# Lightning attention with a leaky-ReLU feed-forward part: a third couple of feature pairs by seven products, and a new order of the group pairs

## The chip, the cores and the metric

The kernel runs on one core of a Trainium2 chip. The metric is the device time of one execution in microseconds; the median of three runs of the kernel before is 598.87 us (598.29 to 600.73).

## What is computed

The reference is an attention with decay, by blocks of 64 positions, whose output goes through two matrix products with a leaky ReLU between:

```python
# q, k, v: (4, 8, 768, 64) float32; lam: (8,)
intra = einsum('bhic,bhjc->bhij', qb, kb) * Dmask        # Dmask = lam ** (i - j) for i >= j
out[:, :, sl] = einsum('bhij,bhjd->bhid', intra, vb) + einsum('bhid,bhde->bhie', qb * lam_pow, kv_state)
kv_state = lam ** 64 * kv_state + einsum('bhsd,bhse->bhde', kb * rev_pow, vb)
...
x = attn_out.transpose(0, 2, 1, 3).reshape(3072, 512)
h = x @ w_in                    # w_in (512, 2048)
out = maximum(0.01 * h, h) @ w_out   # w_out (2048, 512)
```

The two products are 3072x512x2048 and 3072x2048x512. In the kernel each operand of a large product is split into three parts (`h`, `l`, `m`) of a reduced float format, and each product is three passes of TensorE over 128x128 weights and 512 columns.

## The kernel before, in words

**Tiling.** The 3072 tokens are 24 chunks of 128; four chunks are a group (six groups, 0 to 5), two groups are a pair of groups (0-1, 2-3, 4-5; `pr` 0, 1, 2). The 2048 features are eight pairs of 128 (`p` 0 to 7, "feature pairs"); two feature pairs are a couple (`u`: 0 is pairs 0 and 1, 1 is pairs 2 and 3).

**Stages.** The attention's rounds (`round_of`, L552), one a chunk, run between blocks of the first product (`up`, L711; matmuls in L723): a block is one group by one feature pair, 24 matmuls, and ends in ACT passes (L742, L747) into a buffer `gs`. What happens to it then depends on the feature pair. For a *plain* pair the block is written to DRAM (`G`, L754). For a pair that goes *by seven products* `sums` (L777) forms three sums or differences of its token and feature halves on DVE (L783) and writes six kinds of blocks to DRAM (`BB`, L791).

The second product follows, one pair of groups after another. It reads the blocks back as **units** (`unit`, L809): one load of 512 KB by SP (L825), an ACT pass (L828) and two DVE passes (L831, L835) that split 128x1024 values into three parts in one of five **ring slots**. A slot is used again five units later, when PE is done with it. A plain unit (`plain`, L885) is one feature pair of one group, 24 matmuls (L851). By Strassen's scheme (`strassen`, L854) a couple of feature pairs and a pair of groups take seven products of 12 matmuls each, numbered 1 to 7 in the code; a product is one unit. Each product adds into one of four couples of PSUM banks, X, Y, Z or V (`KINDS`, L804); between products ACT copies a couple (`copy_banks`, L958) or ACT and DVE add one to another (`add_banks`, L962; L965, L966), through the staging buffer `w32`. Product 4 has a second load and one more DVE pass (L842, L843) through the same `w32`.

The products need sums of weights: an operand for product 5 stands in the place of a quarter of the weights, and three more for products 6, 7 and 3 stand in "extra" places that the attention's buffers left (`w_sums`, L684; `more`, L670). There is room for those of feature pairs 0 to 3. So before, feature pairs 0 and 1 of the first pair of groups and 0 to 3 of the other two go by seven products (`NS, NS0 = 4, 2`, L203), the rest plain.

**What sets the order.** The work is listed in `seq`, written out by hand; an item's place is its rank. `Plan` then orders each engine's queue at build time from costs and latencies written beside each operation: at each step it takes the operation that can start first, and among equals the one of lowest rank. Units of the second product have their rank lowered by `LEAD` items, so that they are ready ahead. TensorE may take a later item when an earlier one is not ready, as far as the banks allow. All ordinary loads and stores go out on SP in that one order; the output's stores (`store_out`, L951) on ACT's queue, the last ones also on SP. For a pair of groups the list is, with `s(t, u)` for product t of couple u and `n(p, gi)` for a plain unit:

```python
seq += [late[0], s(1, 0), late[1], s(1, 1), ("copy", "Z", "X"), late[2], s(6, 0), late[3], s(6, 1), ("copy", "Y", "Z"),
        s(5, 0), s(5, 1), ("add", "Y", "V"), s(7, 0), s(7, 1), ("add", "V", "Z"),
        s(3, 0), n(4, 0), s(2, 0), n(5, 0), s(3, 1), s(2, 1), n(6, 0), s(4, 0), s(4, 1), n(7, 0)]
```

`late` are the four plain units of the second group of the pair before, moved in between. The last two plain units make the ending (L917).

## Time and profile before

| | |
|---|---|
| median of 3 runs | 598.87 us |
| profiled execution | 598.83 us, of which span 597.1 us |
| granted TensorE clock | 1.0 |
| attention and first product | to 349 us, mixed with the first products of pair 0-1 from 324 us |
| pair 0-1 | last plain units to 437 us, mixed with the first products of pair 2-3 from 413 us |
| pair 2-3 | last plain units to 519 us, mixed with the first products of pair 4-5 from 494 us |
| pair 4-5 | to 592.6 us, then the last stores |
| DMA | 123.04 MB, 206 GB/s over the span |

The page of the profile gives each engine's busy time; its chain of work shows what each instruction on the way to the end waited for. A line such as `437.04 2.77 PE po L851 x12` is start, length, engine, tile written, line of the kernel and count. The names of tiles: `psc` are the banks X, `po` Z, `b` and `pt` are Y and V; `xh`, `xl`, `xm` and `raws` are ring slots, `w` is `w32` or a weight, `att`, `attb` and `lows` are the attention's buffers that later hold sums of weights.

### The profile page before, as it was taken

How to read it: one execution, taken by the hardware profiler on the slowest of the kernel's cores; microseconds unless marked ns; L12 is line 12 of the kernel's file. 1: busy time of each engine (PE TensorE's matmuls, PEld its weight loads, DVE VectorE, ACT ScalarE, POOL GpSimd, SP SyncE). 2: the span in 40 equal slices, each digit the busy share in tenths (PEclk: the TensorE clock that was granted, in tenths of full speed). 3: DMA queues.
4: the chain of work that ended last, by engine and by line, in shares of the span. 5: the costliest groups of instructions: out<-in, count | busy, mean ns of one | idle time of the engine just before them, and what ended most of it. 6: DMA issues, size and time to landing. Idle time of an engine off the chain costs nothing.

```text
span 597.1 us, 13281 instructions
## 1 busy us (share of the span) xinstructions
PE 586.2 (98%) x5336; PEld 485.0 (81%) x5336; DVE 406.7 (68%) x559; ACT 299.2 (50%) x468; POOL 134.0 (22%) x170
## 2 busy tenths in 40 slices
PE   7899999999999999999999999999999999999997
PEld 6778888888888888888788888888888888888886
DVE  4999883357365565465389889965689695788652
ACT  3788884345555565565598874331344223252300
POOL 2654770835636348121000000000000000000000
PEclk9999999999999999999999999999999999999999
DMA  8999855975899999886788865526467547394533
GB/s 205 238 292 242 245 171 132 247 195 132 240 284 260 239 269 232 247 259 224 244 273 273 298 196 206 162 89 190 128 198 223 175 144 193 121 259 164 177 107 70
DMA packets 163949, 123.04 MB, mean 206 GB/s; under 512 B 100400, under 2 KB 140592, under 8 KB 163888
## 3 DMA queue, kind: packets, MB, share of 16 engines
q1 hardware_dynamic: 148128, 112.75, 64.4%
q10 hardware_dynamic: 13200, 5.77, 3.8%
q0 software_dynamic: 2560, 3.68, 2.5%
q8 instruction: 42, 0.69, 0.5%
q14 instruction: 19, 0.16, 0.1%
HBM read 81.27 MB, written 40.89 MB: 205 GB/s over the span
## 4 chain that ended last, share of the span: by engine, by line
PE 91%; DVE 5%; DMA 2%; ACT 0%; issue 0%; SPq 0%; DVEq 0%
PE b L723 43%; PE po L851 13%; PE b L851 12%; PE psc L851 11%; PE pt L851 4%; PE po L335 4%; PE psc L335 3%; DMA xm<-g 1%; DVE wl L628 1%; DVE w L617 1%; DMA attb<-in_q_dram 1%; DVE w L616 1%; PE pt L425 1%; DVE att L474 0%; DVE xl L530 0%
## 5 line engine op out<-in xcount | busy, mean ns | idle before, releaser
L723 PE MATMUL b<-xh,wh 128*128 128x512 f32 (+2 forms) x392 | 103.6, 387 | 0.8 <-ACT xh L529 0.8
L723 PE MATMUL b<-xm,wm 128*128 128x512 f32 (+2 forms) x392 | 103.7, 393 | 0.0
L723 PE MATMUL b<-xl,wl 128*128 128x512 f32 (+2 forms) x392 | 103.5, 386 | 0.1
L828 ACT ACTIVATE xh<-xm 128x1024 fp32r<-128x1024 f32 x46 | 48.8, 1060 | 86.6 <-DMA xm<-g 40.9
L723 PEld LDWEIGHTS b<-xh,wh 128*128 128x128 f32 x392 | 72.7, 188 | 16.1 <-ACT xh L529 0.9
L723 PEld LDWEIGHTS b<-xl,wl 128*128 128x128 f32 x392 | 72.8, 188 | 15.2 <-DVE wl L628 0.5
L723 PEld LDWEIGHTS b<-xm,wm 128*128 128x128 f32 x392 | 71.2, 188 | 15.1 <-ACT b L742 0.4
L742 ACT ACTIVATE b<-b 128x512 f32<-128x512 f32 (+2 forms) x97 | 56.1, 581 | 54.5 <-PE b L723 54.4
L747 ACT ACTIVATE gs<-b 128x512 f32<-128x512 f32 (+2 forms) x97 | 56.8, 591 | 39.7 <-PE b L723 34.6
L831 DVE SCALAR_TENSOR_TENSOR xl<-xm,xh 128x1024 fp32r<-128x1024 f32 x46 | 56.0, 1218 | 26.4 <-ACT xh L828 25.5
L835 DVE SCALAR_TENSOR_TENSOR xm<-xl,xh 128x1024 fp32r<-128x1024 f32 x50 | 61.2, 1224 | 3.5
L484 POOL TENSOR_TENSOR att<-att 128x256 f32<-128x256 f32 x40 | 34.9, 873 | 37.9 <-DVE att L481 37.9
L616 DVE TENSOR_SCALAR w<-w 128x512 int32<-128x512 int32 x32 | 22.6, 706 | 27.2 <-ACT w L610 27.1
L396 POOL DMA_DIRECT2D attb<-in_q_dram x64 | 39.5, 624 | 2.9 <-issue 1.4
L445 POOL TENSOR_TENSOR att<-att 128x512 f32<-128x512 f32 (+1 forms) x20 | 24.9, 1244 | 63.4 <-PE po L335 47.4
L441 POOL TENSOR_TENSOR attb<-attb,att 128x512 f32<-128x512 f32 (+1 forms) x23 | 26.1, 1136 | 34.6 <-PE po L425 10.5
L851 PE MATMUL psc<-xm,wm 128*128 128x512 f32 x84 | 32.8, 391 | 0.1
L851 PE MATMUL psc<-xh,wh 128*128 128x512 f32 x84 | 32.7, 389 | 0.0
L851 PE MATMUL psc<-xl,wl 128*128 128x512 f32 x84 | 32.7, 389 | 0.0
L474 DVE TENSOR_TENSOR att<-psc,att 128x512 f32<-128x512 f32 x24 | 16.5, 688 | 21.9 <-PE psc L335 21.8
L617 DVE CUSTOM_DVE_ANT_0 w<-w,lows 128x1024 uint16<-128x1024 uint16 x32 | 26.2, 818 | 7.1 <-ACT lows L614 6.2
L828 ACT ACTIVATE raws<-raws 128x1024 fp32r<-128x1024 f32 x12 | 12.7, 1061 | 27.6 <-DMA raws<-g 18.1
(184 smaller groups left out, 1096.3 us busy)
## 6 DMA issues: line engine op xcount, KB each, us to landing
xm<-b SPq DMA_DIRECT2D x28, 512.0 KB, 3.8
g<-gs SPq DMA_DIRECT2D x27, 512.0 KB, 4.6
xm<-g SPq DMA_DIRECT2D x22, 512.0 KB, 4.2
b<-gs SPq DMA_DIRECT2D x20, 512.0 KB, 3.9
raws<-in_moe_w_in_dram SPq DMA_DIRECT2D x16, 512.0 KB, 5.2
raws<-in_moe_w_out_dram SPq DMA_DIRECT2D x16, 512.0 KB, 4.9
attb<-in_k_dram SPq DMA_DIRECT2D x48, 128.0 KB, 4.7
attb<-in_v_dram SPq DMA_DIRECT2D x24, 256.0 KB, 4.7
```

The source lines that it names most:

```text
L335: nc.tensor.matmul(dst[HALF[cols]], lhsT=lhsT[HALF[rows]], rhs=rhs[HALF[rows]], start=start, stop=True, skip_group_check=True)
L396: (move if nm == "k" else carry)(0.55 if nm == "k" else QSL, lambda o=o, z=z, e=nc.sync if nm == "k" else nc.gpsimd: e.dma_start(out=o.rea ...
L484: add("POOL", 0.7, lambda new=new, j=j: nc.gpsimd.tensor_tensor(state[(j + 1) % 4], new, _bc(lam_c, 2, D), op=ALU.mult), [f"st{j % 4}", "f ...
L616: add("DVE", 0.42, lambda: nc.vector.tensor_scalar(d, d, 3, None, op0=ALU.logical_shift_left), [], [key])
L617: add("DVE", 1.0, lambda: nc.vector.tensor_tensor(d, d, low, op=ALU.add), [kl], [key])
L723: nc.tensor.matmul(dst, lhsT=w[z][:, kk * 2 * P + f * P:kk * 2 * P + (f + 1) * P], rhs=x[z][:, kk, toks], start=start and kk == 0, stop=kk ...
L742: add("ACT", ns, lambda b=b: nc.scalar.activation(out=b, in_=b, func=AF.Copy, bias=0.0, scale=S + 1.0), [], [kb], rank=-1.5)
L747: add("ACT", t, lambda o=o, x=s_: nc.scalar.activation(out=o, in_=x, func=AF.Prelu, bias=0.0, scale=(1.0 + 1.0 / S) / (WS * U), alpha=0.01 ...
L828: nc.scalar.activation(out=ring[j][0], in_=g(), func=AF.Copy, bias=0.0, scale=NEAR)
L831: nc.vector.scalar_tensor_tensor(ring[j][1], g(), 1.0, ring[j][0].bitcast(F32), op0=ALU.mult, op1=ALU.subtract)
L835: nc.vector.scalar_tensor_tensor(m, l.bitcast(F32), -S, h.bitcast(F32), op0=ALU.mult, op1=ALU.add)
L851: nc.tensor.matmul(dst, lhsT=lhs(z), rhs=ring[j][z][:, col:col + n], start=first and z == 0, stop=z == 2, skip_group_check=True)
```

## The change

Three things are changed.

1. In one pair of groups, 2-3, three couples (feature pairs 0 to 5) go by seven products: `NSP = [2, 6, 4]`. Feature pairs 6 and 7 stay plain.
2. The pairs of groups are worked through in the order 0-1, 4-5, 2-3, so that this pair comes last. The sums of weights of feature pairs 4 and 5 are formed during pair 4-5 (`w_apart`, items `wq`), in a ring slot, and written to DRAM (`ES`). In the last pair they are fetched (`fetches`, items `wd`) into places whose last use is over: the first weight quarter of feature pairs 0 to 3 (after product 1), one extra place (after product 6), two unused ends of the extra buffers, and the quarter of feature pairs 4 and 5 themselves that product 5 replaces (after their late plain units). Each fetch is 128 KB; there are 24.
3. `seq`, the order of the feature pairs in `up`, and the planner's constants are new.

```diff
     NS, NS0 = 4, 2
+    NSP = [2, 6, 4]
...
-    LEAD = 8.0
+    LEAD = 6.0
...
-    HOLD, WPR, WSR, LEAD0 = 0.15, 2.0, 0.0, 12.0
+    HOLD, WPR, WSR, LEAD0 = 0.6, 8.0, 8.0, 10.0
...
+    ES = {p: dram.tile([P, 6 * d_model], F32, name=f"es{p}", tag=f"es{p}") for p in range(NS, max(NSP))}
...
+    def apart(z, p, k):
+
+        if p == NS or k == 0:
+            return W[k if p == NS else 3][z][:, :NQ]
+        if k == 2:
+            return more(z, 0)[:, :NQ]
+        return extra["lows"][:, 3 * NQ:] if z == 2 else extra["attb"][:, NB - (2 - z) * NQ:NB - (1 - z) * NQ]
+
+    def w_apart(p):
+
+        nonlocal n_ring
+        j, n_ring = RING[(n_ring - len(slots)) % NR], n_ring + 1
+        k, r = ["w320", "w321"], [f"r{z}{j}" for z in "hlm"]
+        add("DMA", 1.5, lambda: nc.sync.dma_start(out=w32f, in_=WO[p]), [f"WO{p}0", f"WO{p}1"], k)
+        b = [w32f[:, i * NQ:(i + 1) * NQ] for i in range(4)]
+        for o, x, y, op in ((3, 1, 3, ALU.add), (1, 0, 1, ALU.subtract), (0, 3, 0, ALU.subtract), (2, 2, 0, ALU.subtract)):
+            add("DVE", 0.42, lambda o=o, x=x, y=y, op=op: nc.vector.tensor_tensor(b[o], b[x], b[y], op=op), [], k)
+        add("ACT", 1.05, lambda: nc.scalar.activation(out=ring[j][0], in_=w32f, func=AF.Copy, bias=0.0, scale=NEAR / S), k, r[:1])
+        add("DVE", 1.25, lambda: nc.vector.scalar_tensor_tensor(ring[j][1], ring[j][0].bitcast(F32), -S, w32f, op0=ALU.mult, op1=ALU.add),
+            k + r[:1], r[1:2])
+        add("DVE", 1.25, lambda: nc.vector.tensor_tensor(ring[j][2], ring[j][1].bitcast(F32), ring[j][0].bitcast(F32), op=ALU.subtract), r[:2], r[2:])
+        add("ACT", 1.06, lambda: nc.scalar.activation(
+                out=ring[j][2], in_=ring[j][2].bitcast(F32), func=AF.Copy, bias=0.0, scale=1.0 / (S + 1.0)), [], r[2:])
+        for z in range(3):
+            add("DMA", 1.5, lambda z=z: nc.sync.dma_start(out=ES[p][:, z * 2 * d_model:(z + 1) * 2 * d_model], in_=ring[j][z].bitcast(F32)), r[z:z + 1], [f"ES{p}{z}"])
+
+    def fetch(p, k, to, writes):
+        for z in range(3):
+            add("DMA", 0.5, lambda z=z: nc.sync.dma_start(out=to(z).bitcast(F32), in_=ES[p][:, (z * 4 + k) * NQ:(z * 4 + k + 1) * NQ]),
+                [f"ES{p}{z}"], [w.format("hlm"[z]) for w in writes])
+
+    def fetches(i):
+
+        if i == 2:
+            for p in (NS, NS + 1):
+                fetch(p, 3, lambda z, p=p: W[p][z][:, NQ:2 * NQ], [f"w{{}}{p}"])
+            return
+        for p, k in ((4, 0), (5, 0), (4, 1), (5, 1), (4, 2)) if i == 0 else ((5, 2),):
+            fetch(p, k, lambda z, p=p, k=k: apart(z, p, k), [f"E{p}{k}{{}}"])
...
-            for i, f in enumerate(fs if p < (NS if g > 1 else NS0) else [None]):
+            for i, f in enumerate(fs if p < NSP[g // 2] else [None]):
...
-    ORDER = [4, 0, 3, 7, 2, 6, 5, 1]
+    ORDER = [0, 3, 2, 7, 1, 5, 4, 6]
...
-    for pr in range(NG // 2):
+
+    for pr, before in ((0, None), (2, 0), (1, 2)):
...
+            if pr == 2:
+                seq += [
+                    late[0], late[1], s(1, 0), ("wq", 4), s(1, 1), ("copy", "Z", "X"), late[2], late[3], s(6, 0), s(6, 1),
+                    ("copy", "Y", "Z"), s(5, 0), s(5, 1), s(7, 1), ("add", "Y", "V"), s(7, 0), s(2, 1), ("add", "V", "Z"),
+                    n(4, 0), s(3, 0), n(5, 0), s(3, 1), s(4, 1), s(2, 0), n(6, 0), s(4, 0), n(7, 0), ("wq", 5)]
+            else:
+                seq += [
+                    late[2], late[1], s(1, 0), s(1, 1), s(1, 2), late[0], late[3], ("wd", 0), ("copy", "Z", "X"), s(5, 0),
+                    s(6, 2), s(6, 1), s(5, 1), ("wd", 2), s(6, 0), s(5, 2), ("copy", "Y", "Z"), ("wd", 1), ("add", "Y", "V"),
+                    s(7, 2), s(7, 0), s(7, 1), s(2, 0), ("add", "V", "Z"), n(6, 0), s(3, 0), s(3, 2), s(2, 1), s(4, 0),
+                    s(2, 2), s(3, 1), s(4, 2), s(4, 1), n(7, 0)]
...
-            put(("up", NG - 1, 2), ("ws", 0))
+            put(("up", NG - 1, 1), ("ws", 0))
             put(("up", NG - 1, 2), ("ws", 1))
-            put(("up", NG - 1, 6), ("fr",))
+            put(("up", NG - 1, 4), ("fr",))
```

The list of the first part of `seq` is new too: up to `("wi", 3)` it is the old one; after it the weights of feature pair 4 come earlier, those of 7 and 0 a little later, and some blocks of `up` change places. The plain units of pair 0-1 also stand in another order.

More of the change, by code (lines that the diff above doesn't have):

```diff
@@ L667, in operand @@
             return W[p][z][:, t * NQ:(t + 1) * NQ]
-        return more(z, p)[:, (-1 - t) * NQ:-t * NQ]
+        return more(z, p)[:, (-1 - t) * NQ:-t * NQ] if p < NS else apart(z, p, -1 - t)
     def more(z, p):
@@ L750, in up @@
         plan.ahead = 0.0
-        if p >= (NS if g > 1 else NS0):
+        if p >= NSP[g // 2]:
             d = G[g // 2][p].rearrange("p (f h g t) -> p f h g t", f=2, h=2, g=2)
@@ L881, in strassen @@
         begins = pr == 0 and t == 1
-        add("PE", 0.227 * (13 if begins else 12), go, [f"r{z}{j}" for z in "hlm"] + [f"{'w' if w >= 0 else 'e'}{z}{p}" for z in "hlm" for p in ps_],
+        add("PE", 0.227 * (13 if begins else 12), go, [f"r{z}{j}" for z in "hlm"] + [f"w{z}{p}" if w >= 0 else f"e{z}{p}" if p < NS else f"E{p}{-1 - w}{z}" for z in "hlm" for p in ps_]
+            + [x + z for x in (["E40", "E41", "E42", "E50"] if t == 1 and u < 2 else ["E52"] if t == 6 and u == 0 else []) for z in "hlm"],
             ACC[d] + (ACC["Z"] if begins else []))
@@ L994, in n @@
             return ("n", r, p, gi) if p < NP - 1 else ("l", r, p, gi, (0, 1, 2, 3) if gi == 0 else (2, 3, 0, 1))
-        late = [n(p, 1, pr - 1) for p in range(NS, NP)] if pr else []
+        late = [n(p, 1, before) for p in range(NS, NP)] if pr else []
         if pr:
-            seq += [late[0], s(1, 0), late[1], s(1, 1), ("copy", "Z", "X"), late[2], s(6, 0), late[3], s(6, 1), ("copy", "Y", "Z"),
-                    s(5, 0), s(5, 1), ("add", "Y", "V"), s(7, 0), s(7, 1), ("add", "V", "Z"),
-                    s(3, 0), n(4, 0), s(2, 0), n(5, 0), s(3, 1), s(2, 1), n(6, 0), s(4, 0), s(4, 1), n(7, 0)]
+            if pr == 2:
[9 more added lines that the diff above has]
+                    s(2, 2), s(3, 1), s(4, 2), s(4, 1), n(7, 0)]
         else:
@@ L1046 @@
             w_sums(x[1])
+        elif x[0] == "wq":
+            w_apart(x[1])
+        elif x[0] == "wd":
+            fetches(x[1])
         elif x[0] == "fr":
```

15 lines of the change are left out of this document (8 added, 7 removed), and 5 rows, old and new, of the table seq.

## Prediction

> **What bounds the kernel now.** I read the page's busy shares first, then the table of windows, then PE's waits, then the chain of work in order of time, and last the DVE and SP timelines of one pair of groups.
>
> ```profile
> PE 586.2 (98%) x5336; PEld 485.0 (81%) x5336; DVE 406.7 (68%) x559; ACT 299.2 (50%) x468; POOL 134.0 (22%) x170
> ```
>
> PE is nearly always busy, but a mean says nothing of stages. The table of windows does (columns: window, its length, busy us of PE, PEld, DVE, ACT, POOL with counts, granted clock, DMA share, GB/s):
>
> ```profile
> 0.00:35.00 35.00, 29.46 (x654) 23.47 (x654) 26.45 (x53) 20.57 (x37) 15.98 (x22) 1.00 0.91 228
> 35.00:60.00 25.00, 24.56 (x354) 19.98 (x348) 23.93 (x32) 21.26 (x37) 12.07 (x10) 1.00 0.98 266
> 60.00:292.00 232.00, 232.00 (x3000) 193.46 (x2998) 129.23 (x233) 129.97 (x230) 106.00 (x140) 1.00 0.81 223
> 292.00:360.00 68.00, 67.60 (x311) 55.43 (x312) 56.38 (x75) 55.89 (x86) 0.00 (x0) 1.00 0.82 269
> 360.00:437.04 77.04, 77.04 (x341) 63.79 (x340) 58.20 (x61) 25.07 (x29) 0.00 (x0) 1.00 0.48 149
> 437.04:518.80 81.76, 81.76 (x361) 67.60 (x361) 62.52 (x59) 27.48 (x30) 0.00 (x0) 1.00 0.59 180
> ```
>
> From 60 us to the last pair PE is full: 232.00 of 232.00, 77.04 of 77.04, 81.76 of 81.76. All the room there is before the end lies ahead of 35 us (5.54 us), in 35 to 60 (0.44) and in 292 to 360 (0.40). PE's waits say what it is:
>
> ```profile
> PE psc L335 <- DVE att L481: 1.8, 2, 1.1
> PE b L282 <- POOL att L285: 1.4, 1, 1.4
> PE b L723 <- ACT xh L529: 0.8, 1, 0.8
> PE po L425 <- DVE xl L530: 0.7, 1, 0.7
> ```
>
> These are start-up waits of the attention part. So the kernel is bound by the number of matmuls; anything on another engine is free as long as PE does not wait for it.
>
> **The removed work.** The chain in order of time shows one product of the seven (12 matmuls of 128x512) and two of them in a row:
>
> ```profile
> 437.04 2.77 PE po L851 x12
> ...
> 445.25 5.49 PE po L851 x24
> 450.74 2.72 PE b L851 x12
> ```
>
> A product is 2.72 us, 0.2267 us a matmul. Before, feature pairs 4 and 5 of groups 2 and 3 take 2 x 2 plain units of 24 matmuls: 96, or 21.76 us. After, they are a third couple in each of the seven products: 7 x 12 = 84, or 19.04 us. **12 matmuls less: -2.72 us.** Nothing else on PE changes in number: the other couples, the `up` blocks, the two extra zeroing matmuls of the first product and the ending stay. The saving cannot fail to exist; it can only be eaten by waits.
>
> Beside this row the Trainium skill ("Perfetto Trace Analysis", Identifying the Most-Contended Engine) calls matmul busy time a bad measure and wants the share of weight loads, here 81%. Read so, PE would have 19% room and twelve matmuls might vanish in it (a rival below). The trace speaks against it: a load takes 0.188 us and the next matmul starts 0.2267 us after the last, and 0.188/0.2267 is 83%, so the 81% is that ratio and not idle time.
>
> **The added work, and what hides it.** A "unit" is one 128x1024 operand: one 512 KB load, one ACT pass (1.06 us, L828), two DVE passes (1.22 each, L831 and L835), into one of five ring slots. The last pair has 7 x 3 + 4 = 25 units instead of 22, and three of product 4 (one more load and one more DVE pass, 1.22).
> - DVE, last pair with the four late units before it: 27 units x 2.44 = 65.9, product 4 3 x 1.22 = 3.7, the two bank sums 4 x 0.69 = 2.8, eight output transposes 5.6: 78.0 us, beside PE's 21 x 2.72 + 6 x 5.44 = 89.8. That is 87%, where the pair at 437 us has 62.5 of 81.8 (76%). Hidden on the whole.
> - The weight sums (`w_apart`, twice, in the pair before): 4 x 0.42 + 2 x 1.22 = 4.1 us of DVE, 2.1 of ACT, one load and three stores of 512 KB, and a ring slot each. DVE there becomes 62.5 + 8.3 = 70.8 of 81.8. The slot is held about load 5.4 + DVE and ACT 6.2 + store 4.6 = 16 us; four units stand before its next user, two of them plain ones of 5.44, so 16.3 us. Cost taken: 0; without that cover about one unit's latency less the rest, some 2 us.
> - Sums of activations: 3 x 0.42 us of DVE (L783) for four more blocks in groups 2 and 3, 5 us in a stage where DVE is busy 129 of 232. They stand ahead of the attention's own DVE steps, which have 11 us of other PE work in each round to hide in. Cost 0; upper bound 5.
> - `up` order, ranks and the order of pairs (0-1, 4-5, 2-3): same instructions. Before 35 us the order is the same. After it, it can win at most the 0.44 + 0.40 us of idle time, and it can lose: in 320 to 330 DVE is busy 9.83 of 10 us. I take 0, bounds -0.8 and +3.
>
> **Long runs of products.** The pair now has ten products in a row (from product 5 of couple 0 to product 2 of couple 0), one plain unit, then eight. In a run each unit must be ready within four products, 10.88 us from the release of its slot. The six-run before shows it for product 3 (its load, its two passes with a bank sum between, from the SP and DVE timelines; PE starts it at 450.74):
>
> ```profile
> 439.84 0.32 SPq L825 DMA_DIRECT2D raws<-b  x1
> ```
> ```profile
> 445.07 1.22 DVE L831 SCALAR_TENSOR_TENSOR raws<-raws 128x1024 fp32r<-128x1024 f32 x1
> 446.20 1.29 DVE L966 TENSOR_TENSOR b<-b,w 128x512 f32<-128x512 f32 x2
> 447.40 1.21 DVE L835 SCALAR_TENSOR_TENSOR raws<-raws 128x1024 fp32r<-128x1024 f32 x1
> ```
>
> Ready at 448.61, 8.77 us after its load was issued, 2.1 us to spare. In the run of ten DVE needs 10 x 2.44 + 2.8 = 27.2 us and PE 27.2: no room, but up to four units (9.8 us of DVE) are ready when it begins. The plain unit gives 3.0 back. The run of eight needs 8 x 2.44 + 3.7 = 23.2 against 21.8. From the first run to the last product: DVE 19 x 2.44 + 2.8 + 3.7 + 2.8 (late transposes) - 9.8 = 45.9, PE 51.7 to the start of the last product. It fits, with 5.8 us over.
>
> **Product 4 three times.** All three go through one staging buffer (w32), and the last two stand side by side. Before, the second one's load went out at 470.48 and its last pass ended at 481.64: 11.2 us, without hurry; its bare steps (load 4.9, ACT 1.06, three DVE passes) make 9.6. Counted from the end of the run of ten: the slot of the middle one comes free at 10.9 (plain unit, two products), its second pass ends at 10.9 + 3.8 + 1.22 + 1.06 + 1.22 = 18.2; the last one is then ready at 27.8 to 29.4. PE would want it at 5.44 + 7 x 2.72 = 24.5, or 27.2 once half of the plain unit behind it has gone ahead, as the trace of before has it (psc at 480.71 ahead of po at 483.43). The ending's first halves, 5.4 us on other banks, can go ahead too. So 0, at most 2.2 us.
>
> **The 24 fetches** (128 KB each) have no row of their own. The nearest are the loads of k, 128 KB: 0.59 us of SP (0.37 to 2.34), 4.6 us to land; and four output stores of 128 KB issued within 2.42 us. Fifteen of them may start when product 1 of couple 1 is done; product 6 of the new couple needs the first six 2.72 + 5.44 + 5.44 + 2.72 = 16.3 us later. All fifteen at 0.59 and the landing are 13.5 us: hidden. The load of a unit that queues behind them at that point has 16.3 - 8.8 = 7.5 us to spare, against 8.9 for all fifteen; I take 0, bounds 0 and, in the run itself, 8.9 - 2.1 = 6.8. That a place is freed by region and not by whole tensor I read from the attention part, where DVE and POOL write one part of `att` while PE reads others.
>
> **Sum:** 598.83 (the profiled execution: span 597.1 and 1.7 around it; 0.04 below the median of 598.87) - 2.72 + 0 = **596.1 us**, -0.45%. About 0.5% (3.0 us, so 595.9 to 601.9) is what a measurement can tell from no change, and this saving lies just inside it.
>
> **Rivals.**
> - *The saving stands, up to 1.2 us of new waits* (the forecast): 595.9 to 597.3. For it: PE full through 500 us with the same five slots, and every sum above fits. 0.55.
> - *The new order also closes idle places*: at most 0.84 us, down to 595.3; for it the new ranks at 292 to 360, against it that 0.4 and 0.4 in small pieces are hard to get. 0.16.
> - *The runs outpace the splits*: DVE at 100% in the run of ten, w32 late by 2.2 in the run of eight; 1.2 to 4 us, about 598.3. For it the 2.1 us of slack, against it the units ready beforehand. 0.13.
> - *PE has room* (weight loads 81%): nothing is won, 598.8. Against it the even 0.2267 us. 0.02.
> - *Fetches ahead of loads, slower than before*: SP issues in one order, so if the fifteen fetches come between two loads of the run instead of beside the late plain units, each costs 0.59 and the next unit is 8.9 - 2.1 = 6.8 us late: 602.9. All of the gain is gone from (2.1 + 2.72)/0.59 = 8 fetches in front of one load. For it: their place in the order is behind the late units; against it: they can start 13.6 us earlier, and a free queue takes them then. The same loss would come if the handover at 320 to 350 us, with DVE full, slipped by one unit's latency of 8.8 us. 0.14.
>
> Faster by over 0.5%: 0.16; within: 0.55 + 0.13 + 0.02 = 0.70; slower: 0.14. The range leaves out the slower rival and little else: 595.0 to 601.0.
>
> **What would show it.** Right: about 12 fewer matmuls at L851's form, PE full from 60 us to the last pair, DVE near nine tenths in the last pair, no wait of PE on DVE, ACT or DMA there. The runs: PE waits on L835's form of xm in the last 50 us. The fetches: SP's issues of 128 KB between two unit loads later than product 5. Wrong altogether: idle places of PE between 290 and 360 us longer than 1 us, or PE's start later than now.

## The result, and the profile after

The changed kernel takes **608.58 us** (median of 5 runs, 607.46 to 609.45) where the kernel before takes 598.87 (598.04 to 600.73, 5 runs): a ratio of **1.0159, 95% interval 1.0136 to 1.0181**. The forecast was 596.1, at most 601.0. The profiled execution took 608.12 us, its span is 606.3. Lines of the changed kernel lie 42 higher from the second product on: L851 is now L893, L828 L870, L831 and L835 L873 and L877, L951 L994; L723 is L765.

The page's busy shares first:

```profile
PE 585.8 (97%) x5324; PEld 480.4 (79%) x5324; DVE 429.7 (71%) x592; ACT 302.3 (50%) x473; POOL 133.1 (22%) x170
```

PE has the 12 matmuls less (5336 to 5324). Its last matmul ends at 598.40 us all the same, where it was 592.63: 2.7 us of work went and 8.5 us of waiting came. The table of windows (columns as before) shows that the waits are in nearly every stage that used to be full:

```profile
60.00:294.00 234.00, 232.09 (x2963) 192.59 (x2954) 136.80 (x249) 129.44 (x231) 104.42 (x140) 1.00 0.82 229
294.00:362.00 68.00, 67.73 (x312) 55.16 (x313) 55.83 (x72) 51.92 (x81) 0.00 (x0) 1.00 0.79 255
362.00:442.00 80.00, 79.17 (x349) 65.03 (x348) 63.99 (x69) 26.29 (x30) 0.00 (x0) 1.00 0.55 175
442.00:521.00 79.00, 77.04 (x335) 62.48 (x335) 60.06 (x58) 26.84 (x29) 0.00 (x0) 1.00 0.69 224
521.00:598.40 77.40, 75.66 (x342) 62.34 (x341) 60.26 (x59) 25.02 (x28) 0.00 (x0) 1.00 0.63 197
```

PE's waits, beside the start-up ones that were there before (waiter, line, releaser, sum, times, longest):

```profile
PE b L765 <- ACT gs L789: 1.8, 1, 1.8
PE b L893 <- DVE gs L986: 1.7, 1, 1.7
PE b L893 <- DVE xm L877: 1.7, 2, 0.8
...
PE po L893 <- DVE xm L877: 0.7, 1, 0.7
```

The first is at 158 us, in the first product; the second at 595 us, in the ending; the others at 425, 448 and 510 us, where a unit is split too late. And the end itself is longer: from PE's last matmul to the end of the span it is 7.9 us, before 4.4. ACT's queue shows why (first the kernel before, then the changed one, from 572 and 584 us to the end):

```profile
572.90 21.11 ACTq L951 DMA_DIRECT2D out_dram<-gs  x16
```
```profile
592.20 10.63 ACTq L994 DMA_DIRECT2D out_dram<-gs  x16
```

Before, the eight 128 KB stores of the last pair's first group go out from 572.90 on, while PE works off two plain units and the ending. Now they begin at 592.20, and the ending's stores stand behind them.

**How the runs below are compared.** From each trace I took PE's start-to-start spacing over its regular value (0.2268 us at 512 columns), summed it by stretch, and subtracted the kernel before. "Behind PE" is the time from the last matmul to the span's end, less the 4.4 us of before. The stretch ahead of 60 us is left out: it differs by some 3 us between profiles, also of kernels that are alike there. The column 60-200 hangs on how the small matmuls of the attention are counted: other countings of the same traces give 2.2 to 2.8 us where the table has 3.4 for the changed kernel, and 1.9 to 2.4 for its 2.8 of two couples. Which kernels lose more there is roughly the same by each; its sizes are good to about 1 us. Time and ratio are of all the runs, the stretches of one profiled execution, which can lie 3 us off its kernel's median.

| kernel | median us | ratio to before | 60-200 | 400-470 | 470-525 | 525-550 | 550 to PE's end | behind PE |
|---|---|---|---|---|---|---|---|---|
| changed | 608.58 | 1.0159 [1.0136, 1.0181] | 3.4 | 2.6 | 1.7 | 0.1 | 2.2 | 3.5 |
| all stores on POOL | 614.55 | 1.0229 [1.0184, 1.0274] | 4.8 | 2.2 | 2.5 | 0.0 | 4.7 | 3.4 |
| end buffer | 608.40 | 1.0159 [1.0132, 1.0186] | 2.4 | 1.9 | 1.9 | 0.1 | 0.8 | 4.4 |
| both | 609.95 | 1.0188 [1.0151, 1.0224] | 2.5 | 2.3 | 4.5 | 0.1 | 1.7 | 4.9 |
| no fetches | 608.49 | 1.0151 [1.0133, 1.0168] | 2.8 | 2.3 | 1.9 | 0.1 | 3.0 | 1.9 |
| small weight stores | 609.50 | 1.0171 [1.0137, 1.0206] | 1.2 | 0.3 | 5.0 | 0.1 | 2.3 | 3.2 |
| stores not from the slot | 612.43 | 1.0208 [1.0184, 1.0233] | 2.6 | 0.0 | 7.7 | 0.0 | 2.3 | 3.4 |
| first group earlier | 606.38 | 1.0127 [1.0090, 1.0164] | 3.2 | 2.1 | 1.9 | 0.0 | 1.0 | 1.6 |
| two couples last | 604.55 | 1.0080 [1.0049, 1.0111] | 2.8 | 0.7 | 0.0 | 2.1 | 0.0 | 0.0 |
| order of pairs alone | 598.60 | 0.9995 [0.9982, 1.0008] | 0.4 | 0.0 | 0.0 | 0.0 | 0.0 | 0.0 |
| plain block second | 609.98 | 1.0177 [1.0150, 1.0204] | 2.7 | 2.8 | 1.6 | 0.0 | 2.5 | 3.6 |
| ... and end order | 606.77 | 1.0134 [1.0104, 1.0163] | 2.4 | 1.6 | 1.5 | 0.4 | 1.1 | 1.9 |
| ... and half of the stores on POOL | 605.27 | 1.0096 [1.0071, 1.0121] | 2.9 | 2.3 | 2.2 | 0.1 | 1.8 | 1.3 |
| couple's moves on POOL | 611.23 | 1.0187 [1.0151, 1.0224] | 3.1 | 3.6 | 2.6 | 1.0 | 2.8 | 3.1 |
| ... and plain block between | 610.63 | 1.0174 [1.0143, 1.0204] | 0.8 | 3.1 | 0.5 | 1.7 | 2.7 | 3.0 |
| ... and end order | 608.19 | 1.0138 [1.0122, 1.0153] | 1.1 | 3.9 | 2.9 | 1.7 | 1.2 | 1.3 |
| ... and no bytes of the couple | 608.48 | 1.0132 [1.0096, 1.0168] | 2.2 | 0.0 | 6.9 | 0.1 | 1.6 | 1.3 |
| ... and last store off ACT | 601.51 | 1.0039 [1.0014, 1.0063] | 2.8 | 0.8 | 0.7 | 1.1 | 1.2 | 1.1 |
| two couples, block between | 603.02 | 1.0047 [1.0032, 1.0062] | 1.1 | 0.8 | 0.0 | 2.0 | 0.0 | 0.1 |

### The profile page after: what moved, and what is told of

It is laid out like the page before. It is cut to its first block, busy times and chain, and to the rows that moved or that the text cites. A ratio compares the mean times of both kernels' runs of the same rounds, so it can differ in the third digit from the quotient of the medians.

```text
span 606.3 us, 13372 instructions
## 1 busy us (share of the span) xinstructions
PE 585.8 (97%) x5324; PEld 480.4 (79%) x5324; DVE 429.7 (71%) x592; ACT 302.3 (50%) x473; POOL 133.1 (22%) x170
## 4 chain that ended last, share of the span: by engine, by line
PE 76%; DVE 10%; DMA 7%; issue 2%; ACTq 1%; SPq 1%; ACT 1%; POOL 0%; DVEq 0%
PE b L765 39%; PE po L893 12%; PE psc L893 9%; PE b L893 8%; PE po L337 3%; PE psc L337 3%; PE pt L893 2%; DMA out_dram<-gs 2%; ACTq L994 1%; DVE xl L873 1%; DMA b<-gs 1%; DVE w L619 1%; DVE gs L986 1%; DVE w L618 1%; DMA attb<-in_q_dram 1%
## 5 line engine op out<-in xcount | busy, mean ns | idle before, releaser
L765 PE MATMUL b<-xh,wh 128*128 128x512 f32 (+2 forms) x392 | 103.9, 388 | 2.6 <-ACT gs L789 1.8
L765 PE MATMUL b<-xm,wm 128*128 128x512 f32 (+2 forms) x392 | 104.3, 393 | 0.0
L765 PE MATMUL b<-xl,wl 128*128 128x512 f32 (+2 forms) x392 | 103.6, 387 | 0.2
L765 PEld LDWEIGHTS b<-xh,wh 128*128 128x128 f32 x392 | 72.6, 188 | 18.7 <-ACT gs L789 2.7
L765 PEld LDWEIGHTS b<-xl,wl 128*128 128x128 f32 x392 | 72.8, 188 | 15.6 <-DVE wl L630 1.0
L765 PEld LDWEIGHTS b<-xm,wm 128*128 128x128 f32 x392 | 70.7, 188 | 15.9 <-ACT b L784 1.5
L870 ACT ACTIVATE xh<-xm 128x1024 fp32r<-128x1024 f32 x46 | 48.8, 1060 | 61.7 <-DMA xm<-g 16.7
L873 DVE SCALAR_TENSOR_TENSOR xl<-xm,xh 128x1024 fp32r<-128x1024 f32 x46 | 56.1, 1219 | 25.4 <-ACT xh L870 25.3
L877 DVE SCALAR_TENSOR_TENSOR xm<-xl,xh 128x1024 fp32r<-128x1024 f32 x52 | 63.7, 1224 | 4.0
L486 POOL TENSOR_TENSOR att<-att 128x256 f32<-128x256 f32 x40 | 33.0, 825 | 40.4 <-DVE att L483 38.6
L618 DVE TENSOR_SCALAR w<-w 128x512 int32<-128x512 int32 x32 | 20.4, 636 | 25.0 <-ACT w L612 24.9
L893 PE MATMUL psc<-xm,wm 128*128 128x512 f32 x80 | 31.3, 391 | 0.2 <-DVE xm L877 0.2
L893 PE MATMUL psc<-xh,wh 128*128 128x512 f32 x80 | 31.2, 389 | 0.0
L893 PE MATMUL psc<-xl,wl 128*128 128x512 f32 x80 | 31.1, 389 | 0.0
L893 PE MATMUL b<-xm,wm 128*128 128x512 f32 x72 | 28.3, 393 | 1.7 <-DVE xm L877 1.7
```

The source lines that it names most:

```text
L486: add("POOL", 0.7, lambda new=new, j=j: nc.gpsimd.tensor_tensor(state[(j + 1) % 4], new, _bc(lam_c, 2, D), op=ALU.mult), [f"st{j % 4}", "f ...
L765: nc.tensor.matmul(dst, lhsT=w[z][:, kk * 2 * P + f * P:kk * 2 * P + (f + 1) * P], rhs=x[z][:, kk, toks], start=start and kk == 0, stop=kk ...
L870: nc.scalar.activation(out=ring[j][0], in_=g(), func=AF.Copy, bias=0.0, scale=NEAR)
L873: nc.vector.scalar_tensor_tensor(ring[j][1], g(), 1.0, ring[j][0].bitcast(F32), op0=ALU.mult, op1=ALU.subtract)
L877: nc.vector.scalar_tensor_tensor(m, l.bitcast(F32), -S, h.bitcast(F32), op0=ALU.mult, op1=ALU.add)
L893: nc.tensor.matmul(dst, lhsT=lhs(z), rhs=ring[j][z][:, col:col + n], start=first and z == 0, stop=z == 2, skip_group_check=True)
```

## The experiments

### Which part of the change costs what: two couples last, order of pairs alone

The first takes back the third couple (`NSP = [2, 4, 4]`, no `wq` and `wd`, the last pair's list as before) and leaves the new order of blocks, ranks and pairs, with the planner's constants and the new lists of pairs 0-1 and 4-5:

```diff
-    NSP = [2, 6, 4]
+    NSP = [2, 4, 4]
...
```

> The third couple is taken back: pairs 4 and 5 of the last pair of groups are plain units again, nothing is stored or fetched for their weights, and 12 matmuls come back; the order of the up blocks, the ranks and the order of the pairs of groups (2 and 3 last) stay as changed. Theory (the couple with its stores, its long runs and its lost plain units costs all but the wait at 158 us): about 599 + 1.5 = 600.5 us, with the wait at 158 us still there. Rival (the new order of blocks and pairs costs as much as the couple): 604 or more. If the wait at 158 us comes from the sums of pairs 4 and 5, it goes and the time is about 599.

The second is the kernel before with nothing but the new order of the pairs of groups:

```diff
-    for pr in range(NG // 2):
+    for pr, before in ((0, None), (2, 0), (1, 2)):
...
```

> The kernel before with one edit: the pairs of groups come in the order 0 and 1, 4 and 5, 2 and 3; blocks, ranks, two couples in each and the order inside a pair stay as before. The run with two couples last measured 604.6 us, 5 above before. Theory (these 5 us come from the new order of the up blocks and the new ranks, lead 6 in place of 8 above all): 599 to 600 us here, with no wait of PE over 1 us after 150 us. Rival (the order of the pairs makes them, through the output stores among the last pair's loads): 601.5 or more, with a wait near 537 us.

Measured: 604.55 and 598.60 us. The order of the pairs is free (0.9995). The new order of the blocks with its ranks, constants and lists costs 0.8%, nearly 5 us, with no third couple at all; which of these four costs how much was not taken apart. The couple adds another 0.8%. Both guesses of the first expectation fell short: 604.55 lies in the rival's field. In the table the 0.8% are 2.8 us in 60-200 (the wait at 158 us and small ones) and 2.7 us after 400, at 455 and 537 us. The wait at 158 us is there without the sums of feature pairs 4 and 5, so these don't make it.

The wait at 537 us can be read line by line, since the last pair's list is the same in the two kernels. ACT's queue in the second (order alone; start, length, line, what), where the next unit's first pass (L828) finds its way between the last four stores:

```profile
529.49 0.32 ACTq L951 DMA_DIRECT2D out_dram<-gs  x1
529.85 1.06 ACT L828 ACTIVATE xh<-xm 128x1024 fp32r<-128x1024 f32 x1 [2.42 <-DMA xm<-g]
529.88 1.50 ACTq L951 DMA_DIRECT2D out_dram<-gs  x3
```

And in the first (two couples last), ACT, then SP:

```profile
531.49 3.11 ACTq L994 DMA_DIRECT2D out_dram<-gs  x3
534.64 1.06 ACT L870 ACTIVATE xh<-xm 128x1024 fp32r<-128x1024 f32 x1 [6.05 <-DMA out_dram<-gs]
```
```profile
528.95 0.53 SPq L867 DMA_DIRECT2D xm<-g  x1
```

The trace names a completion semaphore for each transfer of SP and ACT, eight in turn for the two queues together. The third of these stores has the semaphore of SP's load of 528.95; that load lands at 534.25, and the store goes out at 534.28. The unit whose load landed at 531.47 waits behind it until 534.64. So a store waits for a load that it has nothing to do with, ACT stands in the store, and PE waits for the split. The other kernel has such a wait too, and there it is free: its store of 529.49 has the semaphore of a load that landed at 529.46, but that is the load of the very unit that ACT splits next (529.85).

### The output stores on POOL, and the ending's buffer

```diff
-            add(e, 0.5, lambda a=a, q=q: store(a, q), ...
+            add(e, 0.5, lambda a=a, q=nc.gpsimd if len(cs) == 4 else q: store(a, q), ...
```

> The changed kernel with the same order on every engine, except that the 40 output stores that stood in ACT's queue are issued from POOL's queue, which has no work by then. Theory (stores): in the changed kernel ACT's splits wait behind output stores that themselves wait for earlier transfers to land, and the short products leave no cover; PE's new waits at 425, 449, 455 and 510 us (1.0 + 0.8 + 0.3 + 1.6) vanish, and part of the late end goes too: 602.5 to 605 against 608.6. Rival (fetches): the waits come from the 24 fetches ahead of loads on SP, which stay: 608 to 609. Rival (runs): DVE cannot keep up with the runs of products: 608 to 609, the waits stay where they are.

The second gives the ending an output tile of its own, so that its transposes needn't wait for the first group's stores:

> The changed kernel with the same order on every engine, except that the ending's output tile lies in another buffer, so that its transposes no longer wait for the eight stores of the first group of the last pair. Theory (stores): the wait of PE before its last 12 matmuls (1.9 us) goes, and the 7.9 us from PE's end to the end of the span come near the 4.5 of before, less what the eight stores still hold on ACT's queue: 603.3 to 606.5 against 608.6. Rivals (fetches, runs): their cost lies before the ending, so no more than 0.5 us is won.

> Both edits together: output stores from POOL's queue and a buffer of its own for the ending. Theory (stores): 3.7 us of waits in the middle and 5.3 at the end are gone, and what is left over the forecast is the 2 us wait at 158 us: 598.5 to 601. Rivals (fetches, runs): at least 605.

Measured: 614.55, 608.40 and 609.95 us. With all 128 KB stores on POOL, ACT's queue is free, and it is 6 us slower: the stores no longer wait for anything, go out in a burst, and the unit loads beside them land late (a load issued at 507.20 took 8.6 us). The Trainium skill ("DMA: Bandwidth & Descriptors", Issuing engines are not separate DMA queues) says that all queues end on the same 16 engines and that another issuing engine saves only issuing time; this run agrees. The buffer takes the wait at 595 us away (1.9 us) and gains nothing: the span's end is then held by the stores alone (8.8 us behind PE instead of 7.9). It is the lateness of the first group's stores that costs, not the buffer.

### The fetches left out

```diff
+            ... if (p, k) == (5, 1) else None
```

> The changed kernel with the same order on every engine, with 21 of the 24 fetches left out (the products of the third couple then read other numbers; the output of groups 2 and 3 is not the reference's). Theory (stores): the fetches are hidden; 607.5 to 609 against 608.6. Rival (fetches): without them the loads come in time and the waits from 425 us on go as far as they are theirs: 602 to 605.

Measured: 608.49. The 24 fetches are hidden, as forecast, and the rival that put them ahead of the loads falls.

### The stores of the weight parts: bytes, slot or queue

Three kernels take apart what `w_apart` does to the loads behind it. Fewer bytes:

```diff
-  out=ES[p][:, z * 2 * d_model:(z + 1) * 2 * d_model], in_=ring[j][z].bitcast(F32)
+  out=ES[p][:, z * 2 * d_model:z * 2 * d_model + P], in_=ring[j][z][:, :P].bitcast(F32)
```

> The six stores of the weight parts of pairs 4 and 5 write 128 of 1024 columns each (64 KB in place of 512 KB), and the 24 fetches read the same sizes from the plain weights in memory, so groups 2 and 3 of the output are not the reference's; the order of every engine's instructions and all other work stay. Theory (the stores of the parts, by their bytes or by the time that they hold a slot, make the PE waits near 425, 448, 455 and 510 us): these waits, 3.8 us in sum, go, and the time is about 604.8 us. Rival (the output stores on ACT's queue alone make them): the waits stay within 0.5 us and the time is 608.5. Neither touches the wait at 158 us or the end.

All the bytes, but not from the slot (`in_=W[7][z]` in place of `ring[j][z]`):

> The six stores of the weight parts keep their 512 KB, their place on SP's queue and their target, but read the parts of pair 7, which lie finished, instead of the slot; so the slot comes free without waiting for a store to land, and SP does not wait for the parts to be made. Groups 2 and 3 of the output are not the reference's. Theory (the held slot and SP's queue behind it): the waits near 425 to 455 and 510 us go as in the run with small stores, 604.8 us. Rival (the 3 MB of traffic beside the output stores): the waits stay or move, 607.5 to 609 us.

All the bytes from the slot, but issued by POOL (`nc.gpsimd` for `nc.sync` in the stores of `w_apart` and in `fetch`):

> The changed kernel with the 6 stores and 24 fetches of the third couple's weight parts issued by POOL and not by SP; the same bytes, and the order of PE, DVE and ACT stays. Theory (these transfers hold SP and take places in the rotation of eight semaphores, so that unit loads come late and ACT's output stores wait for young loads): the waits at 425 to 455 and 510 us, 3.9 us in sum, fall under 1 us; 608.6 - 3.5 = 605 us, with the waits at 158 and 595 us left. Rival (their bytes beside the output stores): the waits stay, or the loads land later, 608 or more.

Measured: 609.50, 612.43 and 611.23 us; none is faster. By stretches they do tell apart. The waits of 400-470 us go in the first (0.3) and in the second (0.0), and stay in the third (3.6): so it isn't SP's queue and not the bytes alone, but **the slot that is held until the last store has landed**. The chain of waits of the changed kernel shows it:

```profile
413.09 1.81 ACTq L994
...
415.00 1.07 ACT xm L698
...
416.09 3.92 DMA es<-xm
...
420.02 5.41 DMA xm<-b
...
425.52 1.07 ACT xh L870
```

ACT's last step on the parts (L698) stands behind five output stores, the store of the part behind it, and the next load into this slot goes out 0.01 us after that store has landed. From ACT's first write of the slot (403.25) to there it is 16.8 us: 4.6 us of passes on ACT and DVE, 3.9 of the last store, 2.2 behind the output stores on ACT, and 6.0 in which DVE does other things between ACT's first pass (to 404.32) and its own (L695, 410.33), the four output transposes of the group among them.

But in both kernels that free the slot early the stretch 470-525 grows, from 1.7 to 5.0 and 7.7 us, and eats more than was won. Only the rival that the waits "stay or move" foresaw something of the kind, and not its size. The traces show the mechanism of 537 us again. In the kernel with small stores the last of eight output stores has the semaphore of a unit's load that was issued at 501.56 and lands at 506.40; the store goes out at 506.43, and the next unit's first pass, whose own load had landed at 500.74, comes behind it:

```profile
498.01 8.73 ACTq L994 DMA_DIRECT2D out_dram<-gs  x5
506.87 2.00 ACT L870 ACTIVATE xh<-xm 128x1024 fp32r<-128x1024 f32 x2 [7.80 <-PE psc L893]
```

In the kernel whose stores don't read the slot it is a load landing at 509.07 and a store at 509.10. In the changed kernel the same store has another partner, the couple's own last weight store (issued at 501.88, landed at 507.44; the output store goes out at 507.46), and ACT stands less long. So each of these edits also changes which transfer the last store waits for. In the third kernel the couple's moves run beside the units' loads instead: between 495 and 525 us these take 6.0 to 8.8 us as medians by tile, in the changed kernel 5.0 to 5.7.

### The first group earlier; blocks in another order

Only the last pair's list is changed, so that by the plan the first group is done 11 us before PE's end. (Two of the three product 7s come behind the sum of V and Z there, so the second group lacks their share; the instructions are the same in number.)

> Only the order of the last pair's products from product 7 on is changed, so that the first group of the pair is finished 11 us ahead of PE's end by the plan and not 6, with the same 14 units and the same number of stores. Theory (the first group's eight 128 KB stores come too late and stand behind PE's end): the wait at 595 us goes (-1.9) and the stretch from PE's end to the span's end falls from 7.9 to about 4.4 us (-3.5), against about 1.1 us of new waits on product 4 in the plan: about 604.3 us. Rival (the sixteen stores of the ending set it by themselves): 608.5 to 609.5.

Measured: 606.38 us, 2.2 less than the changed kernel, half of what was expected: the wait at 595 us falls to 0.5, the stretch behind PE to 6.0 us, not to 4.4. The interval overlaps that of the changed kernel; the two further kernels below with such an order go the same way, 0.4% under the ones that they are built on. The first group's stores begin at 586.84, 10 us ahead of PE's end; in the kernel before it is 20 us.

For the wait at 158 us a list was changed:

```diff
-    ORDER = [0, 3, 2, 7, 1, 5, 4, 6]
+    ORDER = [0, 6, 2, 3, 1, 5, 4, 7]
```

> The changed kernel with one list altered: the blocks of groups 2 to 4 come in the order 0, 6, 2, 3, 1, 5, 4, 7 in place of 0, 3, 2, 7, 1, 5, 4, 6, so that the block after the first of group 2 is a plain one (one store to wait for) and not one with sums. Theory (the wait at 158 us comes from a second block with sums whose store stands behind seven other transfers on SP): the wait goes, about 606.6 us against 608.6. Rival (any block there finds SP as full): the wait stays over 1 us, 608 to 609.

609.98 us, and the wait is still 1.55 us: the theory of the second block fell. The next two build on it: the end order again, with all sums in place, and then half of the stores on POOL.

> The run before it in this batch (plain block second) with the last pair's products put in an order in which the first group is finished 11 us before PE's end by the plan, with all sums as they must be (all product 7s ahead of the sum of V and Z). Theory (stores of the first group late): the wait at 595 us goes (-1.9), the stretch behind PE's end falls to 4.4 us (-3.5), the plan's new waits on product 4 cost 1.8: together with the wait at 158 us about 603 us. Rival (product 4's longer chain of two loads costs more than the plan says): the end is gained, but 3 us or more of new waits between 555 and 575 eat it, 605 or more.

> The run before it with half of the 128 KB output stores issued by POOL; plan and order as there. Theory (ACT stands in its stores, which wait for loads in flight, and the next unit's first part waits behind them): the waits near 425, 448 and 510 us fall from 3.7 us in sum to under 2, about 2 us faster than the run before it. Rival (stores that do not wait are in the way of the loads, as in the run with all of them on POOL): loads land later, waits of the same or greater size, 0 to 3 us slower than the run before it.

606.77 and 605.27 us. The end order gains about what it gained alone. Half of the stores on POOL is not worse, as all of them are, and not clearly better: the intervals overlap, and the waits that it was to shorten did not fall (400 to 525 us: 3.1 before this edit, 4.5 with it).

What stands around 158 us is a row of five blocks with sums (1 of group 1 and 0 of group 2 among them) where before a plain block stands between. Their stores `b<-gs` must leave one of the two buffers `gs` before the next block but one can use it. SP in the changed kernel:

```profile
149.75 2.14 SPq L362 DMA_DIRECT2D attb<-in_k_dram  x2
151.94 2.79 SPq L833 DMA_DIRECT2D b<-gs  x1
```

This store, of block 1 of group 1, lands at 159.02, and ACT writes into its buffer at 159.12. The run with the plain block second had cut the row from five to three, and this store and the wait behind it stayed, so the length of the row is not what counts. Putting the plain block 4 of group 1 last among the blocks of groups 0 and 1 puts a plain block's store in that place. The edit was made to the kernel with the couple's moves on POOL and to the one with two couples:

```diff
-           ("r", 10), ("up", 1, 2), ("up", 1, 4), ("r", 11), ("up", 1, 0), ("up", 1, 1)]
+           ("r", 10), ("up", 1, 2), ("up", 1, 0), ("r", 11), ("up", 1, 1), ("up", 1, 4)]
```

> The run before it with the last four blocks of groups 0 and 1 in another order: block 4 of group 1, a plain one, comes last and not third, so that blocks 1 of group 1 and 0 of group 2, both with sums, do not follow each other, and only four blocks in place of five with sums stand in a row around it. Theory (the row of blocks with sums fills SP's queue): the wait at 158 us goes, 2 us faster than the run before it. Rival (the wait moves to the next pair of blocks with sums): no faster.

> The kernel with two couples in the last pair and the changed block order (604.6 us), with the plain block 4 of group 1 put last among the blocks of groups 0 and 1, as in the run of that name. Theory (the row of blocks with sums makes the wait at 158 us and nothing else): that wait goes, 602.5 us, and the waits at 455 and 537 us, 2.2 us, stay, since the output stores and loads there are not touched. Rival (other costs of the new block order and ranks hold the time): 604 or more.

Measured: 610.63 (before the edit 611.23) and 603.02 (before the edit 604.55); both intervals overlap those without the edit, so the times alone show no gain. The stretch 60-200 falls from 3.1 to 0.8 and from 2.8 to 1.1, of which the wait at 158 us makes 0.9 and 1.4; in the first pair another 1.5 us is a single wait at 63 us, which the edit does not touch. In the thirteen profiles without this edit in which the wait can stand it is 0.6 to 2.0 us, in six of them 1.5 or more; in the five with it 0.0, 0.2, 0.4, 1.2 and 1.3. So the late store of a block with sums is the larger part, not all; in the two profiles in which the wait comes back the plain block's store lands later (at 158.45 and 160.09, in the other three at 156.80 to 157.51), and what delays it stays open. In the two-couple kernel the other two waits stayed as expected, and its chain passes through an output store whose data no engine reads:

```profile
522.54 5.04 DMA xm<-b
...
527.60 4.37 DMA out_dram<-gs
...
531.99 1.23 DVE xl L873
```

### All three, without the bytes, and one store off ACT

> The run before it with the end order of the earlier run (all product 7s ahead of the sum of V and Z, the first group finished 11 us before PE's end in the plan). Theory (three separate costs, which add up): 608.6 - 3.5 - 2 - 3.6 = 599.5 us, as the kernel before; with the rest of the plan's new waits on product 4 mended it would be 1.8 less. Rival (the costs share one cause, the DMA load, and come back elsewhere): 602 or more.

608.19 us: the costs do not add up; what goes in one place comes back after 400 us (3.9 + 2.9 + 1.7 + 1.2 = 9.7 us). Then the couple's bytes are taken from it:

> The run with all three edits (608.2 us), with the stores of the third couple's parts cut to 128 of 1024 columns (64 KB each) and 21 of its 24 fetches left out, the three left reading plain weights; groups 2 and 3 of the output are then not the reference's. All engines but POOL keep their order. Theory (6 MB of transfers beside the output stores, and the slot held until the store has landed, make the waits between 425 and 455, 510 and 520, 533 and 539 us, 8.7 us in the profile of the run with all three edits): most of them go, about 600 us. Rival (the output stores on ACT's queue make them whatever else moves, as in the kernel with two couples): 5 us or more of them stay, 605 or more.

608.48 us, as slow as with them. All waits between 400 and 550 us go but one: 470-525 grows to 6.9 us. ACT's queue and SP's in that place:

```profile
497.85 9.69 ACTq L994 DMA_DIRECT2D out_dram<-gs  x5
507.66 4.15 ACT L870 ACTIVATE xh<-xm 128x1024 fp32r<-128x1024 f32 x4 [8.76 <-DMA xm<-g]
```
```profile
495.96 5.96 SPq L867 DMA_DIRECT2D xm<-g  x2
```

The second load of SP's line goes out at 501.40 and lands at 507.20; the eighth output store has its semaphore, and goes out at 507.22. The unit loaded at 495.96 had landed at 500.51; its first pass comes at 507.66, behind that store. PE stands still but for two single matmuls, and its clock falls (window, busy PE, granted clock, DMA share, GB/s):

```profile
510.00:520.00 10.00, 9.43 (x28) 0.66 0.08 28
```

The last run takes this one store in eight off ACT:

```diff
-  q=q: store(a, q)
+  q=nc.gpsimd if len(cs) == 4 and m == 1 and a == 3 else q: store(a, q)
```

> The run without the couple's bytes (608.5 us), with one more edit: the last of every eight 128 KB output stores is issued by POOL, whose transfers use other semaphores; seven of eight stay on ACT. Groups 2 and 3 of the output are not the reference's, as there. Theory (the last store waits for the load that is the eighth transfer before it, and the next unit's first part stands behind the store on ACT): the wait between 506 and 516 us, 7.0 us with the spacing of 0.43 us behind it, falls under 2 us, and the time to about 603. Rival (the stores' bytes hold the unit's load, whatever queue issues them): the wait stays over 4 us and the time at 606 or more.

**601.51 us, 7 us less** by the medians (5.6 by the ratios, each to the kernel before as measured beside it), with no run of the one in the range of the other, and the stretch falls from 6.9 to 0.7 (1.8 of it comes back in 400-470 and 525-550). ACT there:

```profile
500.35 2.07 ACTq L994 DMA_DIRECT2D out_dram<-gs  x4
503.39 1.06 ACT L870 ACTIVATE xh<-xm 128x1024 fp32r<-128x1024 f32 x1 [1.99 <-DMA xm<-g]
```

Four stores in 2.07 us, and the unit's first pass when its load has landed. The store's bytes still move beside the loads, so the rival falls. This is the clearest result of the study: one store with a shared semaphore cost 6 to 7 us, in a kernel whose couple moved next to nothing. It also sets the rule of the Trainium skill cited above in its place: the time on the issuing engine can be large, where the engine stands in an issue that waits and its next instruction is one that PE waits for. The edit was not tried in the changed kernel itself, where the last store waits for the couple's own store and 1.7 us are at stake.

No version was faster than the kernel before. With the end order, the block between, fewer bytes (and so other outputs) and the last store off ACT it comes to 1.0039 of it, though it has 12 matmuls less. Of the versions with the third couple whose output is the reference's the best is the one with half of the stores on POOL, 1.0096.

## Why the prediction was wrong, point by point

The forecast missed by 12.5 us. By the runs some 4.8 of it came with the new order, without a third couple, and some 7.4 with the couple. The steps in the prediction's own terms:

- **"12 matmuls less: -2.72 us"**: right, 5336 to 5324; PE's sum of waits then ate it three times over.
- **"the ending stay"**: this step failed. The ending's instructions stay, but the two plain units of feature pairs 4 and 5 stood between the first group's last unit and the ending, 10.9 us of cover for eight stores, and they are the work that the change removes. Price: 3.5 us behind PE and 1.9 at 595 us (2.2 in 550 to PE's end). The sum asked what a removed unit gives and not what stood beside it. I even counted on the ending's first halves going ahead of product 4; they did, and so put the first group's outputs behind them.
- **`up` order, ranks: "I take 0, bounds -0.8 and +3"**: this step failed too, beyond its bound: 4.8 us with two couples, part of it in 60-200 us (3.4 us in the changed kernel by the table, 2.8 with two couples), the rest after 400. "Same instructions" was true; that the store of a block with sums now stood where a plain one's had was not looked at, nor SP's queue past which these stores move. The place that I feared, 290 to 360 us, lost nothing (PE is busy 67.73 of 68.00 us in 294 to 362, before 67.60 in 292 to 360).
- **`w_apart`: "the slot is held about ... 16 us; ... 16.3 us. Cost taken: 0 ... without that cover ... some 2 us"**: the hold was 16.8 us, but that the two figures agree is luck. The 16 count 5.4 us of a load that goes to `w32` and not into the slot; without it and DVE's sums on `w32` some 9 us are left, and most of the rest is DVE's other work ahead of L695 (6.0) and the output stores ahead of L698 on ACT (2.2), which the sum had at nothing. The cover did not do: the stretch 400-470 lost 2.6 us, of which 0.7 are there without the couple. It was reckoned to the next load's issue, with nothing left for that load's own landing beside output stores (5.4 us).
- **Activation sums 0**: no run that changes the sums alone was made. The kernel with two couples lacks those of pairs 4 and 5 and has nearly the same loss in 60-200 (2.8 and 3.4).
- **Long runs, product 4, DVE 87%**: right. From 525 us to the ending no wait of 0.4 us; product 4 lost 0.3; DVE was busy 73.9 of 93.2 us between 499.5 and 592.7 (79%), less than forecast.
- **Fetches 0**: right, 608.49 without them. The slower rival had the right sign from a wrong mechanism. Nor did the signs of being wrong name the places: PE's waits on L877's `xm` came at 425 to 510 us and not in the last 50.
- **What no step had**: the output stores on ACT. I wrote of five slots, SP and DVE, and never asked what ACT's queue holds between two first passes of a unit. The trace of before shows the same eight stores without harm to PE. One of them waits for a load there too, which is the next unit's own. In the changed order they wait for younger transfers: for a load at 537 with two couples (2.1 us), for the couple's own weight store at 510 in the changed kernel (1.7), for a load again in the run that shows it alone (6 to 7).

The costs roughly close: the ratio of the changed kernel to the one with two couples is 0.8%, 4.7 us, and 2.72 of saved work make it 7.4 us of the couple's own waits. The table gives 3.5 (behind PE) + 2.2 (550 to PE's end) + 1.9 (400-470, over 0.7) + 1.7 (470-525) - 2.0 (525-550, which the couple's kernel does not have) = 7.3, or 7.9 with the 0.6 by which 60-200 differs. The other 4.8 us are the order's: 2.8 + 0.7 + 2.1 = 5.6 in its profile, the stretch ahead of 60 us left out. Medians stand here against single profiles that can lie 3 us off them, so that it comes out this closely is partly luck.

Open: what decides that the wait at 158 us comes back in two of five profiles; which part of the new order (blocks, ranks, constants, lists) costs what; and whether a list of the last pair exists that keeps all three product 4s, ends its first group 20 us early and leaves ACT's stores no young load to wait for.

## What to carry to other kernels

When work is removed, list what lay beside it: a saved unit may have been the cover of stores, and it is the stores that then set the end. A transfer that nobody waits for still blocks the queue that issues it; where loads and stores share a few completion semaphores, look up which earlier transfer a store waits for, and keep such stores off an engine whose next instruction is on the critical path. A plan that fills PE to the last microsecond on paper has to know landing times and queues; this one counted an output store as 0.5 us of ACT, and ACT stood up to 9.7 us in five of them.

## What the runs showed of the hardware

- In these traces SP's and ACT's transfers take eight completion semaphores in turn, together, and POOL's take others. A store on ACT whose semaphore was last taken by a load waited until the load had landed, to 0.03 us: 534.25 and 534.28, 506.40 and 506.43, 507.20 and 507.22.
- A unit's load of 512 KB takes 4.1 to 4.6 us as a median of the changed kernel, by tile, 5.4 beside output stores (420.02), and 8.6 once when the stores came from POOL in a burst (507.20).
- In the run without the couple's bytes PE lost 4.3 us between 506.4 and 511.4 us, with two single matmuls in between; then its 512-column matmuls came every 0.43 us for 5 us, and the granted clock was 0.66 in the window 510-520. The Trainium skill ("TensorE: Matmul & The Clock Gate", Part 1: The HAM clock gate) says that an idle window throttles the array to half its clock, 426.7 ns a matmul; the spacing agrees, though PE was not wholly idle here. So a long wait costs more than itself: of the 6.9 us, 4.3 are this wait and the rest is the spacing behind it.
